# Two transformer layers on one core: the first weight cast ahead of the turned rows, powers ahead of masks, and the division of one late unit ahead of all else

## The chip, the cores and the metric

The kernel runs on 1 core of one Trainium2 chip (trn2). A core has TensorE (PE, with its weight loads shown apart as PEld), VectorE (DVE), ScalarE (ACT), GpSimd (POOL) and SyncE (SP, which here only issues DMAs). Each of these engines takes its own list of instructions strictly in order; between engines they wait for each other through semaphores. The metric is the device time of one execution in microseconds, the median of several runs.

## The reference

An input of 2048 rows by 640 columns goes twice through attention and a dense block with the same weights:

```python
x = A_x
x = x + _A_ref(_layernorm(x, axis=-1), A_wqkv, A_wo)
x = x + _B_ref(_layernorm(x, axis=-1), B_w1, B_b1, B_w2, B_b2)
x = x + _A_ref(_layernorm(x, axis=-1), A_wqkv, A_wo)
x = x + _B_ref(_layernorm(x, axis=-1), B_w1, B_b1, B_w2, B_b2)
```

`_A_ref` makes q, k and v of 32 heads (20 columns each) with one 640x1920 product, takes a softmax over a causal window of 256 positions, and multiplies the heads' sums by `wo` (640x640). `_B_ref` is a 640x1536 product, a bias, a squared relu, a 1536x640 product and a bias. Everything is float32 outside; the kernel splits each operand of a large product into a high and a low float16 part and adds three products of them (high-high, high-low, low-high).

## The kernel before

**Units.** The rows are cut into 8 groups of 256, so two layers are 16 units, numbered 0 to 15. A unit's attention is worked in 8 quads of four heads; a quad has a pass for the row maxima (L888 or L705, reduced on DVE by L722), a pass of scores (L737 or L842), four exponentials on ACT (L827), masks on POOL (L856, four to a quad) and on DVE (L865, two), and products with v (L933), whose tile is copied out by ACT (L945) and DVE (L948).

**Dense work between quads.** While unit u's quads run, PE fills the time between them with `dense`: the products of unit u-1 that are left (the `wo` product of `stage_o`, the normalisation and turning of `stage_y`, then `stage_f` with 12 chunks of the first product, named `y,w_s`, and four groups of 36 matmuls of the second, named `w_s,hh`) and the q, k, v products of unit u+1. In the last unit, 15, only the rest of unit 14's work is left to fill with; a reserve of it is meant for the time after the last quad, when unit 15's own sums come back from DRAM (`load_o`), are multiplied by `wo` and are normalised.

**What sets the order.** The kernel is scheduled by hand at build time. Every piece of work for ACT ("A"), DVE ("D"), POOL ("G") and SP ("S") is posted as a job with a cost in ns, the jobs that it depends on, and a priority; `post` inserts it in a list sorted by priority (0 first), and `pump` takes the first job of that list that could start within 250 ns of the plan's clock. The plan's clock and the costs are the planner's own guesses; the instructions come out in the order of the plan, and the chip then waits wherever the guess was wrong. PE's order is decided by the same plan: dense work is put in until the plan says that the jobs a quad waits for are done. A job's cost or priority therefore also moves matmuls, far from the place where it was changed. For a DMA, the plan adds a landing time to the transfer (`LAND` 1800 ns, `WLAND` 4500 ns).

**What the change touches.** `load_wq` (L278 to L291) issues nine loads of the 640x1920 weight on SP's queue, and casts each 128 columns to a high part on ACT (L272) and a low part on DVE (L273). `layernorm` (L359 to L381) makes statistics on DVE (L366, L370, L371), a power -0.5 on POOL (L377), and the normalised row on DVE (L379); `split_t` turns the rows on PE (L404) and splits them with a cast on ACT (L390) and a subtraction on DVE (L391). `load_o` (L969 to L1034) reads the sums of a unit back and, for each quarter of its rows, makes a reciprocal (L1017), a product (L1020), a cast on ACT (L1024) and a subtraction (L1027), all named by the tiles `ov` and `od` in the last two units. The product with `wo` needs the first two quarters for its first 30 matmuls and the last two for the other 30; L1056 adds its result to x.

**PSUM.** The tiles `acc`, `tr` and `pv` of PE share two buffers (`mm_tile`, tag "mm"), taken in turn: a new one waits until ACT or DVE has read the tile before last. At the kernel's start and in unit 15, the turned rows use the banks of the quads (`bb`) instead.

Of the kernel before, what the change touches and what calls it, by code (L numbers as in the profile page):

```python
# [14 lines left out]
ALU = mybir.AluOpType  # L15

P = 128
Q = P // 2
S = 2048
D = 640  # L20
# [6 lines left out]
NU = NL * NG  # L27
KC = D // P
# [17 lines left out]
def kernel(ctx: ExitStack, tc: tile.TileContext, x, wqkv, wo, w1, b1, w2, b2, out):  # L46
# [60 lines left out]
    def set_row(i, k):  # L107
        nc.vector.memset(krow[i][:, 512 * k:512 * (k + 1)], PAIR)
# [8 lines left out]
    LOOK, LAT, LAND, CROSS, WLAND = 250.0, 50.0, 1800.0, 3600.0, 4500.0  # L117
# [27 lines left out]
    def post(eng, cost, fn, *deps, wait=0.0, prio=1, **kw):  # L145

        j = Job(eng, cost, fn, [d for d in deps if d is not None], now[0] + wait, prio, **kw)
        k = len(pend)
        while k and pend[k - 1].prio > prio:
            k -= 1  # L150
        pend.insert(k, j)
        return j
# [5 lines left out]
    def dma(fn, size, *deps, n=1, cost=450.0, prio=1, **kw):  # L158

        return post("S", n * cost, fn, *deps, prio=prio, size=size, **kw)  # L160
# [109 lines left out]
    def convert(st, hi, low, n, load, *deps, prio=2):  # L270

        a = post("A", 20 + 0.9 * n, lambda: nc.scalar.activation(hi, st, AF.Copy, scale=WS), load, *deps, prio=prio)  # L272
        return post("D", 30 + 1.04 * n, lambda: nc.vector.scalar_tensor_tensor(low, st, WS, hi, op0=ALU.mult,  # L273
                                                                               op1=ALU.subtract), a, prio=prio)
# [3 lines left out]
    def load_wq():  # L278
        at = 0
        for lo, n in [(j * D + c, min(2 * P, D - c)) for c in (0, 2 * P, 4 * P) for j in range(2)] + [  # L280
                (2 * D + c, min(2 * P, D - c)) for c in (0, 2 * P, 4 * P)]:
            raw, o = (w1raw, at) if at + KC * n <= FC * D else (krow[2], at - FC * D)
            at += KC * n
            st = raw[:, o:o + KC * n].rearrange("p (c n) -> p c n", c=KC)
            load = dma(lambda st=st, lo=lo, n=n:
                       nc.sync.dma_start(st, wqkv[:, lo:lo + n].rearrange("(c p) n -> p c n", p=P)),
                       P * KC * n * 4, prio=0, land=WLAND)
            for z in range(0, n, P):
                c = slice(lo + z, lo + z + P)
                wqj[(lo + z) // P] = convert(st[:, :, z:z + P], wq_s[:, 0, :, c], wq_s[:, 1, :, c], KC * P, load,  # L290
                                             prio=1)  # L291

    rowset = {}

# [64 lines left out]
    def layernorm(src, y, *deps, prio=2):  # L359

        box = {}

        def stats(i):
            if i == 0:
                box["st"] = sb.tile([P, 2, 6], F32, name="bst", bufs=2)
            nc.vector.bn_stats(box["st"][:, i, :], src[:, i * HD:(i + 1) * HD])  # L366

        def var():
            box["mv"] = mv = sb.tile([P, 4], F32, name="bmv", bufs=2)
            nc.vector.bn_aggr(mv[:, 0:2], box["st"])  # L370
            nc.vector.tensor_scalar(mv[:, 2:3], mv[:, 1:2], 1e-5, YS ** -2, op0=ALU.add, op1=ALU.mult)  # L371

        j = None
        for i in range(2):
            j = post("D", 455, lambda i=i: stats(i), j, *(deps[i:i + 1] or deps), prio=prio)
        j = post("D", 400, var, j, prio=prio)
        j = post("G", 520, lambda: nc.gpsimd.tensor_tensor(box["mv"][:, 3:4], box["mv"][:, 2:3], neghalf,  # L377
                                                                   op=ALU.pow), j, prio=prio)
        j = post("D", 576, lambda: nc.vector.tensor_scalar(y, src, box["mv"][:, 0:1], box["mv"][:, 3:4],  # L379
                                                           op0=ALU.subtract, op1=ALU.mult), j, prio=prio)  # L380
        return j  # L381
# [34 lines left out]
    def xsrc(l, b):  # L416
        return x_rows[b * P:(b + 1) * P, :] if l == 0 else xs[b]
# [7 lines left out]
    def ln_load(u, *deps, prio=2):  # L425

        l, g = divmod(u, NG)
        ys = []
        for i in range(2):
            xt = sb.tile([P, D], F32, name="xt", tag="xt", bufs=2)  # L430
            load = dma(lambda xt=xt, i=i: nc.sync.dma_start(xt, xsrc(l, 2 * g + i)), P * D * 4, *deps, prio=min(prio, 1))
            ys.append((xt, layernorm(xt, xt, load, prio=prio)))
        lns[u] = ys
# [535 lines left out]
    def load_o(u, late=False, free_=()):  # L969

        l, g = divmod(u, NG)
        opened0.clear()
        if late:
            val = sb.tile([P, KC, T], F32, name="ov", tag="qt", bufs=2)
            od = sb.tile([P, KC, 2, T], F16, name="od", tag="yT", bufs=1)
        else:
            raw = sb.tile([P, 2, KC, T], F32, name="od", tag="hh", bufs=1)
            val = raw[:, 0]
            od = raw[:, 1].rearrange("p c n -> p (c n)").bitcast(F16).rearrange("p (c a n) -> p c a n", a=2, n=T)
        wrote = [ojobs.pop((u, qd)) for qd in range(1, NQ, 2)]  # L980
        rs = sb.tile([P, T], F32, name="rs", bufs=1)

        def load():
            nc.sync.dma_start(rs, ods[u][:, DH:DH + 1].to_broadcast([H, 4, T]))
            nc.sync.dma_start(val.rearrange("p c n -> p (c n)"), ods[u][:, :DH].rearrange("h (d c) n -> h d (c n)", d=4))

        loaded = dma(load, P * (KC + 1) * T * 4, *wrote, *free_, n=2, prio=0)
        if u == NU - 1:
            both = sb.tile([P, 2, D], F32, name="x1", tag="qt", bufs=2)
            x1 = [both[:, i] for i in range(2)]  # L990
        elif u == NU - 2:

            x1 = [krow[(u - 1) % 3][:, i * D:(i + 1) * D] for i in range(2)]
        else:
            x1 = [sb.tile([P, D], F32, name="x1", bufs=2) for i in range(2)]
        xj = {}

        def load_x(i, *deps):
            xj[i] = dma(lambda: nc.sync.dma_start(x1[i], xsrc(l, 2 * g + i)), P * D * 4, *deps, prio=2)

        for i in range(2):

            k = 2 * u + i - 2
            if k < 0 or u >= NU - 2:
                load_x(i, *([loaded] if u == 0 else wrote if u == NU - 1 else ()))
            elif k < len(stored):
                load_x(i, stored[k])
            else:
                waiting[k] = lambda k=k, i=i: load_x(i, stored[k])


        js = []
        for i in range(4):
            q = slice(i * T // 4, (i + 1) * T // 4)

            def ratio(q=q):
                nc.vector.reciprocal(rs[:, q], rs[:, q])  # L1017

            def times(q=q):
                nc.vector.tensor_tensor(val[:, :, q], val[:, :, q],  # L1020
                                        rs[:, q].unsqueeze(1).to_broadcast([P, KC, T // 4]), op=ALU.mult)

            def high(q=q):
                nc.scalar.copy(od[:, :, 0, q], val[:, :, q])  # L1024

            def low(q=q):
                nc.vector.tensor_sub(od[:, :, 1, q], val[:, :, q], od[:, :, 0, q])  # L1027

            pr = urgency["od"]
            j = post("D", 575, ratio, loaded, prio=pr)  # L1030
            j = post("D", 409, times, j, prio=pr)
            j = post("A", 360, high, j, prio=0 if i < 2 else pr)
            js.append(post("D", 402, low, j, prio=pr))
        ols[u] = od, x1, js, xj  # L1034
        if u == NU - 2:
            opened.end = now[0]
        if u == 0:
            rowset[2] = [post("D", 460, lambda k=k: set_row(2, k), *[w2j[c] for c in (7, 8, 9, 10, 11)], prio=2) for k in range(4)]
            for j, load_ in held:
                load_(loaded, *(rowset[2] if j else ()))  # L1040
# [291 lines left out]
    spin(14)  # L1332
    ln_load(0, prio=0)
    load_wq()
    run(ln_t(0))
    spin(7)
# [25 lines left out]
    for n in range(NQ):  # L1362
        todo += [("s", n)] + ([("r", n + LEAD - GQ)] if n % GQ == 1 else []) + [("m", n + LEAD), ("v", n)]
    flow(todo, rest)
    load_o(0)
    dma(lambda: nc.sync.dma_start(b1s, b1.rearrange("(c p) -> p c", p=P)), 8192, *ols[0][2], prio=2)
    b2load = [dma(lambda: nc.sync.dma_start(b2s, bass.AP(tensor=b2.tensor, offset=b2.offset, ap=[[0, P], [1, D]])),
# [60 lines left out]
```

## Time and profile before

| what | value |
|---|---|
| median of 3 runs | 1554.59 us (1553.53 to 1555.71) |
| the profiled execution, its own time | 1555.59 us |
| its span, first to last instruction | 1553.9 us |
| PE busy | 1530.8 us, 25832 matmuls |
| DVE, ACT, POOL busy | 1036.8, 670.0, 453.0 us |
| mean granted clock of PE | 0.998 |

Times in a timeline are microseconds from the span's start; a row gives start, length, engine, line, operation, tiles, and in brackets how long the engine was idle before it and what ended that. In a table of waits a row says who waited for whom, in total, how often, and the longest. In a table of windows each engine's busy time stands with its number of instructions, then the clock that PE was granted (1.00 is full, 0.50 half) and what the DMA engines moved.

### The profile page before, as it was taken

The page shows a single profiled execution, that of the slowest core. Times are in us where ns is not written, and L with a number is a line of the kernel's source. Part 1 is how long each engine was busy: PE and PEld are TensorE (multiplying, and loading weights), DVE is VectorE, ACT ScalarE, POOL GpSimd, SP SyncE. Part 2 cuts the span into 40 slices and gives each one's busy share as a digit, 9 for nine tenths or more (in the row PEclk, how much of TensorE's full clock was granted, in tenths as well). Part 3 has the DMA queues.
Part 4 walks back from the last instruction along what each step waited for, and adds up shares of the span by engine and source line. Part 5 has one row for each costly group of instructions (what it writes and reads, how often), then busy time and mean ns, then how long its engine had stood idle before and what let it go on. Part 6 is the DMA issues. An engine that isn't in the chain of part 4 may idle for free.

```text
span 1553.9 us, 58533 instructions
## 1 busy us (share of the span) xinstructions
PE 1530.8 (99%) x25832; PEld 1197.5 (77%) x25832; DVE 1036.8 (67%) x2246; ACT 670.0 (43%) x1367; POOL 453.0 (29%) x847
## 2 busy tenths in 40 slices
PE   8998999999999999999999999999999999999999
PEld 7766778787787877778777787877878777786777
DVE  8788775666766567665656767667665676767641
ACT  4564445344443534534343443444435345354422
POOL 1223314133231322314132241332314224142321
PEclk9999999999999999999999999999999999999999
DMA  9773353442534334343353434435343352432010
GB/s 283 206 224 100 78 130 86 117 101 80 127 69 125 86 105 114 61 128 79 110 130 65 122 82 130 89 81 128 67 131 79 104 121 62 121 86 64 27 62 18
DMA packets 240343, 162.34 MB, mean 104 GB/s; under 512 B 93016, under 2 KB 224088, under 8 KB 240088
## 3 DMA queue, kind: packets, MB, share of 16 engines
q1 hardware_dynamic: 234136, 149.09, 38.0%
q10 hardware_dynamic: 5952, 9.50, 2.1%
q8 instruction: 203, 3.33, 0.9%
q14 instruction: 52, 0.43, 0.1%
HBM read 79.76 MB, written 58.72 MB: 89 GB/s over the span
## 4 chain that ended last, share of the span: by engine, by line
PE 94%; DVE 3%; ACT 1%; issue 1%; POOL 0%; ACTq 0%; DVEq 0%; POOLq 0%
PE acc L340 74%; PE pv L933 8%; PE bb L705 5%; PE bb L842 5%; PE bb L933 2%; ACT pt L827 1%; DVE mx L722 1%; DVE bb L685 0%; PE bb L737 0%; PE bb L888 0%; DVE bb L719 0%; DVE qd L538 0%; POOL pt L856 0%; PE tr L404 0%; DVE mx L685 0%
## 5 line engine op out<-in xcount | busy, mean ns | idle before, releaser
L827 ACT ACTIVATE pt<-bb 128x640 f32<-128x640 f32 (+2 forms) x512 | 312.5, 683 | 164.7 <-PE bb L842 141.0
L856 POOL TENSOR_SCALAR_AFFINE_SELECT pt<-pt 64x256 f32<-64x256 f32 x448 | 198.5, 443 | 595.9 <-ACT pt L827 566.7
L340 PE MATMUL acc<-y,w_s 128*128 128x256 f16 x2880 | 330.3, 273 | 2.3 <-DVE y L391 2.1
L340 PE MATMUL acc<-w_s,hh 128*128 128x320 f16 (+1 forms) x2340 | 326.7, 297 | 0.1
L340 PEld LDWEIGHTS <-w_s 128*128 128x128 f16 x2880 | 276.2, 98 | 42.1 <-issue 3.2
L340 PEld LDWEIGHTS <-hh 128*128 128x128 f16 x2340 | 222.1, 98 | 86.8 <-issue 0.4
L722 DVE TENSOR_REDUCE mx<-bb 128x4 f32<-128x1024 f32 x224 | 273.1, 1223 | 6.7
L340 PE MATMUL acc<-yT,wq_s 128*128 128x256 f16 x2250 | 259.0, 273 | 2.4 <-DVE mT L797 0.7
L340 PEld LDWEIGHTS <-wq_s 128*128 128x128 f16 x2400 | 229.6, 98 | 36.5 <-issue 3.4
L865 DVE COPY_PREDICATED_SCALAR pt<-drop,zero 128x256 f32 x224 | 99.8, 498 | 138.9 <-ACT pt L827 138.6
L1121 POOL TENSOR_TENSOR r<-r 128x256 f32<-128x256 f32 x192 | 122.6, 659 | 214.6 <-ACT r L1117 212.0
L945 ACT COPY ot<-pv 128x256 f32<-128x256 f32 x128 | 47.7, 372 | 287.5 <-PE bb L933 255.3
L933 PE MATMUL pv<-pt,vt 64*32 64x128 f32 (+5 forms) x3840 | 168.1, 303 | 0.9 <-ACT vt L624 0.9
L1127 DVE TENSOR_TENSOR hh<-r,hh 128x256 f16<-128x256 f32 x192 | 90.5, 484 | 108.7 <-ACT hh L1124 104.3
L933 PE MATMUL bb<-pt,vt 64*32 64x192 f32 (+3 forms) x3584 | 154.6, 302 | 0.4 <-POOL pt L856 0.4
L719 DVE COPY_PREDICATED bb<-maskq,bb 128x256 f32<-128x256 uint16 x224 | 94.0, 424 | 84.8 <-PE bb L705 84.1
L933 PEld LDWEIGHTS pv<-pt,vt 64*32 64x32 f32 (+1 forms) x3840 | 126.1, 106 | 31.5 <-issue 3.3
L340 PE MATMUL acc<-wo_s,od 128*128 128x320 f16 x960 | 139.6, 300 | 2.1 <-ACT od L1024 2.0
L340 PE MATMUL acc<-wq_s,yT 128*128 128x320 f16 x900 | 130.4, 299 | 1.6 <-DVE kt L391 0.5
L1117 ACT ACTIVATE r<-acc,b1s 128x256 f32<-128x256 f32 x192 | 81.2, 477 | 95.3 <-PE acc L340 93.4
L340 PEld LDWEIGHTS <-od 128*128 128x128 f16 x960 | 91.1, 98 | 40.4 <-ACT od L1024 2.3
L933 PEld LDWEIGHTS bb<-pt,vt 64*32 64x32 f32 x3584 | 116.3, 106 | 1.6 <-POOL pt L856 0.9
(105 smaller groups left out, 1444.8 us busy)
## 6 DMA issues: line engine op xcount, KB each, us to landing
o<-ot SPq DMA_DIRECT2D x64, 256.0 KB
qt<-qk SPq DMA_DIRECT2D x30, 480.0 KB
kt<-qk SPq DMA_DIRECT2D x30, 480.0 KB
qk<-qd SPq DMA_DIRECT2D x15, 640.0 KB
od<-o SPq DMA_DIRECT2D x14, 640.0 KB
qk<-yl SPq DMA_DIRECT2D x13, 640.0 KB
xt<-in_A_x_dram SPq DMA_DIRECT2D x16, 320.0 KB
x<-in_A_x_dram SPq DMA_DIRECT2D x16, 320.0 KB
```

The costliest lines, as they stand in the source:

```text
L340: nc.tensor.matmul(acc, lhs(a, c), rhs(b, c), start=(k == 0), stop=(k == 3 * nk - 1))
L705: nc.tensor.matmul(flat[e][rows, o:o + b - a], qt[r, p, i * P + 64 * h:i * P + 64 * (h + 1)], kt[r, p, a + to:b + to], start=True, stop=Tr ...
L719: nc.vector.copy_predicated(wins[:, :, 4 * Q:], later, wins[:, :, :Q])
L722: nc.vector.tensor_reduce(most, wins[:, :, Q:], axis=mybir.AxisListType.X, op=ALU.max)
L827: return lambda: nc.scalar.activation(room_of(box)[:, a:b], bank[:, a:b], AF.Exp, scale=SCALE / (QS * QS))
L842: nc.tensor.matmul(flat[e][h * Q:(h + 1) * Q, c0:c1], kt[r, 2 * qd + j, k0:k0 + Q], qt[r, 2 * qd + j, q:q + c1 - c0], start=True, stop=Tru ...
L856: nc.gpsimd.affine_select(out=m, in_=m, pattern=[[0, 4], [-1 if k else 1, Q]], base=0, fill=0.0, compare_op=ALU.is_gt if k else ALU.is_ge, ...
L865: nc.vector.copy_predicated(m, drop[:, k:k + 1, :].bitcast(mybir.dt.uint16).to_broadcast([P, 4, Q]), zero.unsqueeze(1).to_broadcast([P, 4, ...
L933: nc.tensor.matmul(pv[h][32 * jj:32 * (jj + 1), q0 * Q:(q0 + w) * Q], vf[r, c:c + 32], boxes[e]["pt"][r, a:b], start=(k == 0), stop=(k == ...
L1117: nc.scalar.activation(box["r"], acc[:, f, :], AF.Relu, bias=b1s[:, f0 + f:f0 + f + 1], scale=1.0 / (YS * WS))
L1121: nc.gpsimd.tensor_tensor(box["r"], box["r"], box["r"], op=ALU.mult)
L1127: nc.vector.tensor_sub(hh[:, 1, f, :], box["r"], hh[:, 0, f, :])
```

## The change

Four numbers of the plan are changed. (1) The plan takes the first of the nine weight loads to land 1800 ns after its transfer, not 4500, and the casts of its first 128 columns get priority 0, not 1. (2) The power of every normalisation gets priority 0. (3) In unit 14, the last but one, the products `times` and (4) the casts `high` of the divided sums get priority 0. No instruction's work changes.

```diff
@@ load_wq
-                       P * KC * n * 4, prio=0, land=WLAND)
+                       P * KC * n * 4, prio=0, land=WLAND if at > KC * 2 * P else LAND)
@@
                 wqj[(lo + z) // P] = convert(st[:, :, z:z + P], wq_s[:, 0, :, c], wq_s[:, 1, :, c], KC * P, load,
-                                             prio=1)
+                                             prio=0 if lo + z < P else 1)
@@ layernorm
         j = post("G", 520, lambda: nc.gpsimd.tensor_tensor(box["mv"][:, 3:4], box["mv"][:, 2:3], neghalf,
-                                                                   op=ALU.pow), j, prio=prio)
+                                                                   op=ALU.pow), j, prio=0)
@@ load_o
-            j = post("D", 409, times, j, prio=pr)
-            j = post("A", 360, high, j, prio=0 if i < 2 else pr)
+            j = post("D", 409, times, j, prio=0 if u == NU - 2 else pr)
+            j = post("A", 360, high, j, prio=0 if i < 2 or u == NU - 2 else pr)
```

**At the start, on ACT.** L390 casts the turned rows of unit 0 (out of the banks `bb_143` and `bb_144`), L272 casts weights. Before:

```order
L390 ACT_TABLE_LOAD
L390 CAST yT<-bb_143 128x3x128
L390 CAST yT<-bb_143 128x2x128
L390 CAST yT<-bb_144 128x3x128
L390 CAST yT<-bb_144 128x2x128
L272 ACTIVATE wq_s<-w_s 128x5x128 x6
```

Changed:

```order
L272 ACT_TABLE_LOAD
L272 ACTIVATE wq_s<-w_s 128x5x128 x2
L390 CAST yT<-bb_143 128x3x128
L390 CAST yT<-bb_143 128x2x128
L390 CAST yT<-bb_144 128x3x128
L390 CAST yT<-bb_144 128x2x128
L272 ACTIVATE wq_s<-w_s 128x5x128 x3
```

Both casts of the first weight load now stand ahead of all four casts of the turned rows. On DVE the first low part (L273) likewise stands ahead of the four subtractions L391.

**Unit 14's division, on ACT.** L1024 is the cast of a quarter, L827 an exponential, L945 the copy of a quad's sums. Before:

```order
L1024 CAST od<-ov 128x5x64
L827 ACTIVATE pt<-bb_143 128x640 x2
L1024 CAST od<-ov 128x5x64
L827 ACTIVATE pt<-bb_144 128x640 x2
L1024 CAST od<-ov 128x5x64
L945 COPY ot<-pv 128x256
L827 ACTIVATE pt<-bb_143 128x640 x2
L827 ACTIVATE pt<-bb_144 128x640
L1024 CAST od<-ov 128x5x64
```

Changed:

```order
L1024 CAST od<-ov 128x5x64
L827 ACTIVATE pt<-bb_143 128x640
L1024 CAST od<-ov 128x5x64
L827 ACTIVATE pt<-bb_143 128x640
L827 ACTIVATE pt<-bb_144 128x640
L1024 CAST od<-ov 128x5x64
L827 ACTIVATE pt<-bb_144 128x640
L1024 CAST od<-ov 128x5x64
L945 COPY ot<-pv 128x256
```

All four casts now lie within the exponentials of one quad; the last stood behind three exponentials of the next. From here on the plan also deals PE's dense work out otherwise: before the last quad's `pv` of unit 15 stood 8 matmuls `w_s,hh`, now 48 stand there (8, 8 and 32); between that `pv` and the product with `wo` stood 100 and now stand 96; behind the product with `wo` stood 16, 12 and 8, now none.

**Behind unit 15's product with `wo`, on PE and DVE.** L404 turns the two normalised tiles of unit 15. PE before, around the first of the two:

```order
L340 LDWEIGHTS hh
L340 MATMUL acc<-w_s,hh 128x320
L404 MATMUL bb_143<-ident,xt 128x128 x5
L340 LDWEIGHTS hh
L340 MATMUL acc<-w_s,hh 128x320
```

PE changed:

```order
L340 LDWEIGHTS od
L340 MATMUL acc<-wo_s,od 128x320
L404 MATMUL bb_143<-ident,xt 128x128 x5
L404 MATMUL bb_144<-ident,xt 128x128 x5
L340 LDWEIGHTS w_s
L340 MATMUL acc<-y_28442,w_s 128x256
```

DVE before, from the last addition of that product (L1056) on:

```order
L1056 SCALAR_TENSOR_TENSOR x_28193<-acc,x_28193 128x320
L366 BN_STATS bst<-x_28193 128x6 x2
L370 BN_AGGR bmv<-bst 128x2
L371 TENSOR_SCALAR bmv<-bmv 128x1
L379 TENSOR_SCALAR xt<-x_28193,bmv 128x640
L391 TENSOR_TENSOR y_28428<-bb_143,y_28428 128x3x128
L391 TENSOR_TENSOR y_28428<-bb_143,y_28428 128x2x128
L391 TENSOR_TENSOR y_28428<-bb_144,y_28428 128x3x128
```

DVE changed:

```order
L1056 SCALAR_TENSOR_TENSOR x_28238<-acc,x_28238 128x320
L366 BN_STATS bst<-x_28238 128x6 x2
L391 TENSOR_TENSOR y_28442<-bb_143,y_28442 128x3x128
L391 TENSOR_TENSOR y_28442<-bb_143,y_28442 128x2x128
L370 BN_AGGR bmv<-bst 128x2
L371 TENSOR_SCALAR bmv<-bmv 128x1
L379 TENSOR_SCALAR xt<-x_28238,bmv 128x640
L391 TENSOR_TENSOR y_28442<-bb_144,y_28442 128x3x128
```

The 36 matmuls that stood among the turned rows are gone from here, and the two subtractions of the first tile now stand inside the second tile's normalisation.

**In unit 1 and in the units after it.** POOL takes a power after one, two or three masks of a quad where it came after all four. In unit 1 this also moves DVE and PE: L379 of the second tile now comes ahead of the quad's two L865 (it came behind them, L719 and L273), PE turns that tile ahead of the quad's `pv` (it came behind), and DVE takes L865 twice, L719 and L273 between that L379 and the tile's two L391. In units 2 to 13 the order on PE, ACT and DVE is as it was, but for a handful of rows in unit 2.

## The prediction

> **What bounds the kernel now.** The chain of waits comes first: which engine ends last.
>
> ```profile
> PE 94%; DVE 3%; ACT 1%; issue 1%; POOL 0%; ACTq 0%; DVEq 0%; POOLq 0%
> ```
>
> The path is PE itself. A table of windows over the middle units shows how full it is:
>
> ```profile
> 200.00:1340.00 1140.00, 1138.26 (x19868) 894.11 (x19867) 756.38 (x1595) 482.76 (x987) 336.05 (x624) 1.00 0.41 100
> ```
>
> PE is busy for 1138.26 of 1140 us at full clock (first two numbers, and the 1.00). Four edits that only change an order can win or lose there 1.7 us at most. What can move lies at the start, in units 0 and 1, in the last two units and behind the last product. So the next views are PE's waits, first in 1390 to 1554 us, then in 120 to 146 us:
>
> ```profile
> PE acc L340 <- ACT od L1024: 2.0, 1, 2.0
> PE acc L340 <- DVE y L391: 1.2, 1, 1.2
> PE tr L404 <- DVE x L1156: 0.3, 1, 0.3
> ```
>
> ```profile
> PE tr L404 <- DVE xt L379: 1.2, 1, 1.2
> PE acc L340 <- DVE y L391: 0.9, 1, 0.9
> PE bb L933 <- POOL pt L856: 0.4, 1, 0.4
> ```
>
> Unit 14's wait for the casts `od` (2.0 us) is the one at which edits 3 and 4 aim; the waits for L379 and POOL in unit 1 are those at which the power's priority aims. All six make 6.0 us, 0.4% of the time. Behind unit 15's product with `wo` PE waits for nothing.
>
> The last view is PE's clock, in windows of 3.41 us:
>
> ```profile
> 134.68:138.09 3.41, 1.40 (x35) 1.08 (x36) 2.38 (x4) 0.89 (x3) 3.33 (x5) 1.00 0.50 155
> 138.09:141.50 3.41, 2.80 (x14) 1.94 (x14) 3.38 (x6) 1.50 (x3) 1.14 (x2) 0.50 0.06 23
> ...
> 1431.74:1435.16 3.42, 1.43 (x39) 0.63 (x27) 2.14 (x6) 2.76 (x5) 1.22 (x3) 1.00 0.24 81
> 1435.16:1438.57 3.41, 3.35 (x80) 2.24 (x88) 2.84 (x6) 0.08 (x1) 1.24 (x3) 0.50 0.00 0
> 1451.20:1454.63 3.43, 2.22 (x50) 1.74 (x51) 2.04 (x5) 2.75 (x7) 0.20 (x1) 1.00 0.49 177
> ```
>
> Two windows ran at half clock (0.50), each right behind one in which PE was busy for only 1.40 or 1.43 us; behind the window with 2.22 us the clock stayed. A halved window does half its busy time's work, so these two cost 2.80/2 + 3.35/2 = 3.1 us, as much as half of the waits themselves. So a cluster of about 2 us of idle time can cost up to 1.7 us more, depending on where the grid of windows falls.
>
> **A, the start.** ACT now casts the first weights ahead of the turned rows. Nothing of this part is hidden: PE is waiting.
>
> ```profile
> 0.00:4.00 4.00, 2.57 (x12) 2.57 (x13) 2.90 (x17) 1.28 (x1) 3.13 (x14) 1.00 0.50 161
> 4.00:6.40 2.40, 2.40 (x18) 2.31 (x17) 2.30 (x11) 0.00 (x0) 0.95 (x3) 1.00 0.93 285
> ```
>
> ```profile
> 7.86 0.48 ACT L390 CAST yT<-bb 128x384 f16<-128x384 f32 x1 [5.77 <-PE bb L404]
> 8.96 1.03 ACT L390 CAST yT<-bb 128x256 f16<-128x256 f32 x3 [0.62 <-DVE yT L391]
> 9.87 3.26 ACT L272 ACTIVATE wq_s<-w_s 128x640 f16<-128x640 f32 x5
> ```
>
> ```profile
> 8.37 0.56 DVE L391 TENSOR_TENSOR yT<-bb,yT 128x384 f16<-128x384 f32 x1 [0.31 <-ACT yT L390]
> 10.83 1.55 DVE L273 SCALAR_TENSOR_TENSOR wq_s<-w_s,wq_s 128x640 f16<-128x640 f32 x2
> ```
>
> ```profile
> 11.70 1.48 PE L340 MATMUL acc<-yT,wq_s 128*128 128x256 f16 x12 [0.63 <-DVE wq_s L273]
> ```
>
> When do the weights land? Not before 6.4: up to there 161 GB/s x 4.0 + 285 x 2.4 = 1.33 MB had come in, which is both x tiles (0.66 MB) and the first load (0.66 MB). Not after 9.87, where L272 ran without a wait. I take the middle, 8.2. Two casts then take 2 x 0.63 us (3.26 for five, the last one 0.73), so the first L390 starts at 9.5 instead of 7.86. It ends at 9.98, its L391 at 10.57 (0.56), the other three L390 at 11.62 (1.03), the next L391 at 12.21. The product's second and third matmul need that and start at 12.25 and 12.36; the third stood at 11.70, on L273, which is now long done. **+0.66 us.** The general form is landing + 4.15, so 7.55 breaks even. Bounds: for a landing at 6.4 the tiles' own casts decide, and -0.57 is left (what PE waited for L273, less a short rest); at 9.87 it is +2.33. Behind this PE runs full, so the shift carries through.
>
> **B, unit 1.** POOL takes the power after the first mask.
>
> ```profile
> 132.13 2.93 POOL L856 TENSOR_SCALAR_AFFINE_SELECT pt<-pt 64x256 f32<-64x256 f32 x4 [5.24 <-ACT pt L827]
> 135.15 0.55 POOL L377 TENSOR_TENSOR bmv<-bmv,neghalf 128x1 f32<-128x1 f32 x1
> ```
>
> ```profile
> 132.80 0.88 DVE L865 COPY_PREDICATED_SCALAR pt<-drop,zero 128x256 f32 x2
> 133.58 0.43 DVE L719 COPY_PREDICATED bb<-maskq,bb 128x256 f32<-128x256 uint16 x1
> 133.91 0.87 DVE L273 SCALAR_TENSOR_TENSOR w_s<-kt,w_s 128x640 f16<-128x640 f32 x1
> 135.73 1.14 DVE L379 TENSOR_SCALAR xt<-x,bmv 128x640 f32<-128x640 f32 x1 [0.95 <-POOL bmv L377]
> ```
>
> ```profile
> 558.15:559.45 1.30, 1.30 (x64) 1.08 (x64) 1.00 0.63 122
> ```
>
> The first mask ends near 133.2, the power at 133.75, and L379 near 134.5 instead of 136.87. PE, free at 133.44, waits 1.05 us for it and turns the tile. But then comes `pv`, and its buffer is that of the turned rows, so it waits for the tile's subtraction; ahead of that on DVE now stand L865 twice, L719 and L273, 0.88 + 0.43 + 0.87 us. They end at 136.4, the subtraction at 136.9. `pv` waits 1.7 us, runs unbroken in 1.3 to 1.4 (the window of another unit), and the next product starts near 138.3. Before, it was 138.70 (137.02, plus the turns, plus 0.94). **-0.4 us**, between -1.4 (`pv` has a free buffer) and +0.5 (L865 held up by its exponentials). One wait becomes another.
>
> **Units 2 to 13.** Only POOL's order changes:
>
> ```profile
> 553.41 1.85 POOL L856 TENSOR_SCALAR_AFFINE_SELECT pt<-pt 64x256 f32<-64x256 f32 x4 [2.11 <-ACT pt L827]
> 555.35 0.55 POOL L377 TENSOR_TENSOR bmv<-bmv,neghalf 128x1 f32<-128x1 f32 x1
> ```
>
> The last masks are done at 555.26, and come 0.55 later; `pv` starts at 558.15, so 2.3 us hide it. **0**; without that cover, 0.55 a unit.
>
> **C1, unit 14's `od`.** All four casts go into one quad's exponentials.
>
> ```profile
> 1434.17 0.47 ACT L1024 CAST od<-ov 128x320 f16<-128x320 f32 x1
> ...
> 1442.65 2.49 ACT L827 ACTIVATE pt<-bb 128x640 f32<-128x640 f32 x4 [3.03 <-PE bb L842]
> ```
>
> The fourth cast stood behind three exponentials (1434.17); now it is done before its matmuls are due, and the 2.0 us go. But the exponentials it passes come later, and so do others that the plan moves: the turned rows of `y` now wait for a cast behind three exponentials of about 0.6 us (2.49 for four). Followed through the new order, the cast of the first turned blocks ends some 0.19 + 2.1 + 0.48 us behind the quad's scores and its subtraction 0.56 later, with the handing on 3.4 in all, while PE has eight products (1.1 us), the 0.3 for L1156 and five turns (0.7) to do: it waits some 1.15 (1.0 to 1.4 by what one takes for the handing on). With 0.2 of a `pv` for L865, 0.27 for L1156 and 0.42 of a `pv` for an L391 that comes late with it, I have 2.05 in all, against 2.0 + 0.3 + 1.2 = 3.5 before. **-1.5 us**; between -3.5 (all vanish) and -1.0.
>
> **C2, behind unit 15's product with `wo`.** This is the price. The plan spends its reserve early: 40 more `w_s,hh` before the last `pv`, none of the 36 behind the product.
>
> ```profile
> 1483.62:1497.21 13.59, 13.59 (x106) 9.80 (x101) 5.47 (x13) 1.75 (x5) 0.00 (x0) 1.00 0.45 151
> ...
> 1505.36:1511.35 5.99, 5.99 (x49) 4.67 (x47) 4.06 (x9) 1.33 (x3) 3.99 (x5) 1.00 0.00 0
> ```
>
> ```profile
> 1495.94 0.49 DVE L1027 TENSOR_TENSOR od<-ov,od 128x320 f16<-128x320 f32 x1
> ```
>
> ```profile
> L340 PE MATMUL acc<-w_s,hh 128*128 128x320 f16 x36 | 5.4, 299 | 0.0
> ```
>
> ```profile
> 1505.57 0.49 DVE L1056 SCALAR_TENSOR_TENSOR x<-acc,x 128x320 f32<-128x320 f32 x1 [1.03 <-PE acc L340]
> 1505.97 0.88 DVE L366 BATCH_NORM_STATS2 bst<-x 128x6 f32<-128x320 f32 x2
> ...
> 1507.95 1.14 DVE L379 TENSOR_SCALAR xt<-x,bmv 128x640 f32<-128x640 f32 x1 [0.66 <-POOL bmv L377]
> 1510.97 0.56 DVE L391 TENSOR_TENSOR y<-bb,y 128x384 f16<-128x384 f32 x1 [0.56 <-ACT y L390]
> ```
>
> The first window, from the last `pv` to the product with `wo`, holds 100 `w_s,hh`; with 96 it is 4 x 0.136 = 0.54 us shorter. The second quarter of the divided sums was ready at 1496.43, 0.78 us ahead of need, so still no wait. The second window is the cover: 5.99 us between the end of the `wo` product (1505.36) and `y`, filled by 36 matmuls and ten turned blocks. Without the 36, the chain itself sets the time, counted from that end: addition to 0.70, statistics to 1.49, now two subtractions of the first tile ahead of the rest (0.56 + 0.34) to 2.43, the two short ones to 2.7, power to 3.35, L379 to 4.5 (1.14), turns and casts to 6.05, subtraction to 6.64; `y` runs from about 6.56. PE has only the turns to do, 1.12 us. **+5.4 us of idle time.** Bounds: 4.9 (the 36 x 0.136 us that filled it, nothing added to the chain) and 6.0 (everything in series).
>
> **The clock.** Before lost 3.1 us. Unit 14's cluster shrinks, unit 1's stays at about 2.7, the tail gets a stretch of nearly 4 us idle, behind which one window is halved: 1.7 + 1.7 = 3.4, **+0.3**; one to three halved windows make -2.1 to +2.0.
>
> The Trainium skill, "TensorE: Matmul & The Clock Gate", Part 1, halves the clock only after a whole idle window of some 3.4 us. The trace disagrees, since windows with 1.40 and 1.43 us of work were enough; what the time would be by that rule is rival 1.
>
> **The sum.** Idle 0.66 - 0.4 - 1.5 + 5.4 = 4.2, clock 0.3: +4.5 on the profiled execution's 1555.59 gives 1560.1. That execution lies 1.0 above the median of the runs (1554.59), so the forecast is **1559.1 us**.
>
> **The rivals.** (1) *A halving needs a window that is nearly all idle.* Then neither unit 1 nor, with luck of the grid, the tail is halved: +4.2 - 3.1 = +1.1, 1555.7, no change to be told. Against it stand the rows with 1.40 and 1.43; for it, that there are only two of them. (2) *The 36 matmuls covered little*, the other side: PE came to them because it was their turn, and `y` could have started without them, if the chain behind the product took no longer than the turns, 1.1 us. Then the tail costs nothing and only gains stay: -1.2 idle and -1.7 clock (unit 14's window), 1551.7. It decides below 2.3 us of chain; against it, the rows L1056 to L391 run one after another over 5.4 us in the trace. (3) *The first weights land late*, at 9.87: +2.3 instead of +0.66, 1560.8. The row without a wait allows it; the bytes speak for earlier. (4) *Unit 14's wait is not of the cast's place* but of the reciprocals and sums' landing: its 2.0 and its 1.7 of clock stay, about 1562. Against it, the cast row at 1434.17 right behind exponentials.
>
> **How the numbers follow.** Forecast 0.64, rival 1 0.14, rival 2 0.05, rival 3 0.11, rival 4 0.06. Own range of the forecast 1557 to 1561.5, from tail and clock bounds. The range for 8 in 10 takes in part of rival 1 and of 4: 1555.9 to 1562.3. A measurement here tells 0.2%, 3.1 us, from no change. Faster (below 1551.5) needs most of rival 2: 0.04. Within: rival 1, some of 2, and the forecast's lower end: 0.24. Slower (above 1557.7): 0.72.
>
> **What would show it.** Right: PE idle for some 5 us between the `wo` product and `y` in unit 15, no wait for L1024 in unit 14, the first product's third matmul near 12.4, a `pv` in unit 1 that waits for L391. Wrong: `y` starting within 2 us of the `wo` product's end, halved windows gone from the record, or 2 us idle before unit 14's `od` matmuls as now.

## The result and the profile after

| | before | changed |
|---|---|---|
| median of 5 runs | 1554.97 us (1553.53 to 1558.28) | 1566.54 us (1564.74 to 1567.67) |
| ratio of the runs (the two medians alone give 1.0074) | | 1.0068, 95% interval 1.0055 to 1.0082 |
| span of the profiled execution | 1553.9 us | 1565.1 us |
| mean granted clock (before: 29 runs, taken with the experiments; changed: the five) | 0.995 to 0.999 | 0.992 to 0.995 |

The change makes the kernel slower, as forecast, but by 11.6 us (medians; 11.2 in the profiled executions) and not by 4.5: 1566.54 lies outside the range, 1555.9 to 1562.3.

Where the 11.2 us of span went is seen in a table of windows, five stages of before and then of the changed kernel. The first two numbers are the length of the stage and PE's busy time; their difference is PE's idle time. Before:

```profile
0.00:60.00 60.00, 55.20 (x497) 44.90 (x498) 51.95 (x173) 30.20 (x57) 10.97 (x29) 1.00 0.83 245
60.00:200.00 140.00, 131.18 (x2173) 97.78 (x2172) 108.36 (x236) 72.51 (x147) 43.16 (x80) 0.99 0.57 151
...
1340.00:1470.00 130.00, 125.27 (x2451) 96.00 (x2448) 91.64 (x180) 60.38 (x122) 43.66 (x82) 0.99 0.27 69
1470.00:1553.90 83.90, 80.93 (x854) 64.74 (x853) 28.43 (x65) 24.14 (x56) 19.18 (x33) 1.00 0.12 39
```

Changed:

```profile
0.00:60.00 60.00, 52.97 (x433) 42.28 (x434) 46.41 (x153) 25.05 (x47) 8.88 (x25) 0.94 0.74 232
60.00:200.00 140.00, 131.13 (x2156) 97.65 (x2155) 112.37 (x252) 74.54 (x153) 43.09 (x80) 0.98 0.58 148
200.00:1340.00 1140.00, 1137.88 (x19782) 893.96 (x19780) 752.39 (x1589) 484.38 (x989) 335.90 (x628) 1.00 0.41 100
1340.00:1470.00 130.00, 127.35 (x2534) 98.21 (x2535) 95.09 (x187) 57.37 (x118) 40.32 (x76) 1.00 0.29 75
1470.00:1565.10 95.10, 87.27 (x948) 68.71 (x940) 29.53 (x69) 27.32 (x63) 21.77 (x38) 0.96 0.11 37
```

| stage | PE idle before | changed | difference |
|---|---|---|---|
| 0 to 60 us (start) | 4.80 | 7.03 | +2.2 |
| 60 to 200 (unit 1) | 8.82 | 8.87 | +0.05 |
| 200 to 1340 | 1.74 | 2.12 | +0.4 |
| 1340 to 1470 (unit 14) | 4.73 | 2.65 | -2.1 |
| 1470 to the end | 2.97 | 7.83 | +4.9 |
| sum | | | +5.5 |

The stretches are fixed in time, and the changed kernel runs some us behind in most of them, so a row says where idle time lies rather than what one wait is worth; the sum is free of that. The idle time accounts for 5.5 us, near the forecast's 4.2. The rest is the clock: the column behind the engines fell from 1.00 to 0.94 in the first stage and to 0.96 in the last. The windows of 3.41 us on the grid of this execution show it, for the start and for the tail:

```profile
9.37:12.78 3.41, 1.35 (x11) 1.00 (x10) 2.31 (x5) 2.78 (x8) 0.00 (x0) 1.00 1.10 376
12.78:16.20 3.42, 3.31 (x16) 2.37 (x16) 3.31 (x7) 1.35 (x3) 0.00 (x0) 0.50 1.08 351
36.67:40.09 3.42, 1.11 (x14) 0.79 (x13) 2.11 (x10) 1.25 (x4) 0.00 (x0) 1.00 0.65 168
40.09:43.50 3.41, 2.92 (x15) 1.68 (x12) 3.40 (x18) 0.25 (x1) 0.00 (x0) 0.50 1.06 327
...
1514.65:1518.06 3.41, 0.00 (x0) 0.00 (x0) 2.66 (x7) 0.44 (x2) 1.67 (x3) 1.00 0.00 0
1518.06:1521.48 3.42, 2.25 (x9) 1.57 (x10) 0.95 (x3) 0.75 (x2) 2.40 (x3) 0.50 0.01 2
1521.48:1524.89 3.41, 3.41 (x18) 2.43 (x16) 0.00 (x0) 0.00 (x0) 0.00 (x0) 0.50 0.00 0
```

Six windows ran at half clock: the four above and two in unit 1 (139.08 to 145.90, PE busy for 1.40 and 2.69 us). Half of their busy time is lost: 1.65 + 1.46 + 2.05 + 2.83 = 8.0 us against 3.1 before, **+4.9 us**. With the 5.5 of idle time that makes 10.4 of the 11.2; the other 0.8 is in the lengths of records at full clock and I cannot place it. One execution is a sample of the clock. Over all runs its mean fell from 0.9973 (29 of before) to 0.9936 (the five), an estimate of 0.0037 x 1555 = 5.8 us.

PE's waits, up to 60 us and then from 1400 us on:

```profile
PE tr L404 <- DVE kt L391: 2.3, 1, 2.3
PE acc L340 <- ACT yT L390: 1.6, 1, 1.6
...
PE acc L340 <- DVE yT L391: 0.6, 1, 0.6
```

```profile
PE bb L404 <- DVE xt L379: 3.9, 1, 3.9
PE tr L404 <- DVE y L391: 0.9, 1, 0.9
PE acc L340 <- ACT y L390: 0.6, 1, 0.6
PE acc L340 <- DVE y L391: 0.5, 1, 0.5
PE tr L404 <- DVE x L1156: 0.3, 1, 0.3
PE pv L933 <- DVE y L391: 0.2, 1, 0.2
```

Unit 14's wait for L1024 is gone, the tail has 3.9 + 0.6 + 0.5 us, and at the start stands one that the prediction did not have: 2.3 us for an L391 of unit 1's turned rows (before: 0.7). The chain of waits over that stretch, in order of time, says what it is made of:

```profile
32.44 4.90 DMA qk<-stg
37.34 0.02 issue
37.37 0.41 ACTq L301
...
37.88 0.49 ACT kt L390
38.37 0.02 issue
38.39 0.57 DVE kt L391
38.96 0.04 issue
39.01 0.56 PE tr L404 x3
```

ACT's cast L390 stands behind L301, an instruction by which ACT issues the first load of `wo`. L301 must wait for a semaphore of an earlier transfer (the program gives its DMAs eight semaphores in turn, numbers 101, 102 and 104 to 109 in the trace; here L301 waits for 107, that of a store of `stg`, issued at 32.44, that lands at 37.34). ACT runs in order, so the cast waits too: it starts at 37.88, 1.7 us after ACT's last work. Before, L301 stood one place earlier in ACT's list, was issued at 30.89 and waited for 101, that of a store issued at 26.57; no stall shows there.

### The profile page after: what moved, and what is told of

It is laid out like the page before. It is cut to its first block, busy times and chain, and to the rows that moved or that the text cites. A ratio compares the mean times of both kernels' runs of the same rounds, so it can differ in the third digit from the quotient of the medians.

```text
span 1565.1 us, 58546 instructions
## 1 busy us (share of the span) xinstructions
PE 1536.6 (98%) x25832; PEld 1200.8 (77%) x25832; DVE 1035.8 (66%) x2246; ACT 668.7 (43%) x1367; POOL 450.0 (29%) x847
## 4 chain that ended last, share of the span: by engine, by line
PE 92%; DVE 3%; ACT 1%; issue 1%; DMA 1%; SPq 0%; POOL 0%; ACTq 0%; DVEq 0%; POOLq 0%
PE acc L340 72%; PE pv L933 8%; PE bb L842 5%; PE bb L705 5%; PE bb L933 2%; ACT pt L827 1%; DVE mx L722 0%; DMA w_s<-in_A_wqkv_dram 0%; PE bb L888 0%; PE bb L737 0%; DVE bb L685 0%; DMA qk<-stg 0%; DMA xt<-xs 0%; DVE pt L865 0%; DVE bb L719 0%
## 5 line engine op out<-in xcount | busy, mean ns | idle before, releaser
L827 ACT ACTIVATE pt<-bb 128x640 f32<-128x640 f32 (+2 forms) x512 | 312.3, 684 | 169.4 <-PE bb L842 147.0
L865 DVE COPY_PREDICATED_SCALAR pt<-drop,zero 128x256 f32 x224 | 99.8, 497 | 138.4 <-ACT pt L827 138.3
L933 PE MATMUL pv<-pt,vt 64*32 64x192 f32 (+5 forms) x3840 | 168.0, 304 | 2.6 <-DVE y L391 1.7
L945 ACT COPY ot<-pv 128x256 f32<-128x256 f32 x128 | 47.6, 372 | 281.8 <-PE bb L933 252.9
L719 DVE COPY_PREDICATED bb<-maskq,bb 128x256 f32<-128x256 uint16 x224 | 93.9, 424 | 85.3 <-PE bb L705 84.0
```

The source lines that it names most:

```text
L719: nc.vector.copy_predicated(wins[:, :, 4 * Q:], later, wins[:, :, :Q])
L827: return lambda: nc.scalar.activation(room_of(box)[:, a:b], bank[:, a:b], AF.Exp, scale=SCALE / (QS * QS))
L865: nc.vector.copy_predicated(m, drop[:, k:k + 1, :].bitcast(mybir.dt.uint16).to_broadcast([P, 4, Q]), zero.unsqueeze(1).to_broadcast([P, 4, ...
L933: nc.tensor.matmul(pv[h][32 * jj:32 * (jj + 1), q0 * Q:(q0 + w) * Q], vf[r, c:c + 32], boxes[e]["pt"][r, a:b], start=(k == 0), stop=(k == ...
```

## Experiments

The theories. **Clock and stall:** besides the idle time of the prediction, a nearly idle window costs half of the next one's busy time, and the landing time of edit 1 moves L301 into ACT's way. **Idle time alone** (the prediction's sum): the clock is a small term, and the start costs 0.66 us. Runs of before that were taken with them: median 1555.9 us (29 runs) for the first four, 1556.4 (21) for the next four, 1557.6 (12) for the last three.

### The edits one by one

The first alone:

```diff
-                       P * KC * n * 4, prio=0, land=WLAND)
+                       P * KC * n * 4, prio=0, land=WLAND if at > KC * 2 * P else LAND)
-                                             prio=1)
+                                             prio=0 if lo + z < P else 1)
```

> The first edit alone (landing time and priority of the first weight casts). By the sum of the prediction it costs 0.66 us and nothing behind the first product: about 1555.6 us, no difference from before. By the trace of the changed kernel it costs 4 to 6 us (1559 to 1561): PE's third matmul near 12.9 us, then a wait of over 2 us for an L391 near 39 us, since on ACT the issue of a weight load (L301) that waits for a transfer stands ahead of the cast L390, and halved clock windows near 13 and 40 us.

Measured: 1558.05 us, ratio 1.0017 (1.0006 to 1.0029), +2.6 us, less than the 4 to 6 of the one theory and more than the 0.66 of the other. Its 12 runs reach from 1554.19 (mean clock 0.998) to 1563.86 (0.993). In the profiled execution, one of the shortest, no window was halved at the start; its span of 1554.2 us says little of the others. The waits are there all the same, from 8 to 60 us:

```profile
PE tr L404 <- DVE kt L391: 1.7, 1, 1.7
PE acc L340 <- ACT yT L390: 1.1, 1, 1.1
PE acc L340 <- DVE yT L391: 0.6, 1, 0.6
```

So the two waits of the start are edit 1's. That a window is halved behind them in one run and not in another fits the place of the grid: here the window at the start, 8.50 to 11.91, held 2.21 us of work, in the changed kernel 1.35.

The second alone:

```diff
-                                                                   op=ALU.pow), j, prio=prio)
+                                                                   op=ALU.pow), j, prio=0)
```

> The second edit alone (power of every normalisation at priority 0). By the prediction -0.4 us with the clock unchanged; by the trace of the changed kernel about 0, since unit 1's waits only change place. Both say 1553.5 to 1556.5. If the clusters of idle time in unit 1 halve two windows instead of one, up to 1.5 us more.

Measured: 1556.46 us, ratio 1.0009 (1.0000 to 1.0017). In the profiled execution PE is idle for 8.39 us between 60 and 200 us, against 8.82: the -0.4 of the prediction. But behind the cluster three windows in a row ran at half clock:

```profile
128.84:132.25 3.41, 1.05 (x33) 0.66 (x24) 3.11 (x9) 2.68 (x6) 0.35 (x1) 1.00 0.00 0
132.25:135.66 3.41, 2.52 (x42) 1.91 (x41) 2.59 (x6) 0.51 (x2) 3.12 (x6) 0.50 0.64 192
135.66:139.08 3.42, 1.88 (x49) 1.44 (x56) 2.91 (x4) 0.47 (x2) 3.35 (x4) 0.50 0.30 96
139.08:142.49 3.41, 3.41 (x43) 2.37 (x24) 2.67 (x5) 1.63 (x3) 0.00 (x0) 0.50 0.02 5
```

They cost 3.9 us, against 1.4 in the profile of before. That this is the edit's doing is not shown: in the run with the priority of the casts alone (below), where unit 1's order is that of before, three windows in a row ran at half clock too (134.35 to 144.59, PE busy for 2.60, 2.69 and 3.41 us: 4.4 us). How the grid falls on the same waits makes a difference of this size.

The third and fourth alone:

```diff
-            j = post("D", 409, times, j, prio=pr)
-            j = post("A", 360, high, j, prio=0 if i < 2 else pr)
+            j = post("D", 409, times, j, prio=0 if u == NU - 2 else pr)
+            j = post("A", 360, high, j, prio=0 if i < 2 or u == NU - 2 else pr)
```

> The third and fourth edit alone (products and casts of unit 14's divided sums). By the prediction -1.5 us in unit 14 and +5.4 us behind unit 15's product with wo, with the clock +4 in all (1559). By the trace of the changed kernel -2.5 in unit 14, +5 idle behind that product and 2.8 us of two halved windows there: +5 (1559 to 1561). No L301 stall and no late first product.

Measured: 1561.53 us, ratio 1.0041 (1.0029 to 1.0054). Unit 14's and the tail's waits are those of the full change (0.3, 0.9 and 0.2; 3.9, 0.6 and 0.5), and two windows behind the tail's wait were halved. The three ratios add up to 0.17 + 0.09 + 0.41 = 0.67%, the full change has 0.68%: within the 0.2% or so that the intervals leave, the edits do not work on each other.

### The tail: is it the cover?

The third and fourth edit, with a limit on how far the plan may run ahead of its share of dense work in unit 15:

```diff
-                c = s.go()
+                c = s.go() if ahead < most else None
...
-        together(quads, ahead, dense, cost, share, ..., pace=NQ)
+        together(quads, ahead, dense, cost, share, ..., pace=NQ, most=5000 if last else 1e9)
```

> The third and fourth edit, and a limit on how far ahead of its share the plan may deal out dense work in unit 15, so that 108 w_s,hh stand before the product with wo and 36 (16, 12 and 8) behind it, as many as before the change. If the 36 matmuls are the cover whose loss costs the time, the wait of some 5 us and the halved windows behind the product go, and unit 14's gain is left: about 2 us faster than before (1552 to 1553.5). If the normalisation is late for another reason, a wait of several us stays and the time is 1558 or more.

Measured: 1557.40 us, ratio 1.0009 (1.0000 to 1.0018): 4.1 us less than without the limit. The tail's wait is gone (PE idle for 3.3 us from 1470 us on, as against 8.3 in the third run and 3.0 before), and so are its halved windows. The kernel did not become the expected 2 us faster than before, since the limit also holds dense work back near 1440 us: 4 products `w_s,hh` instead of 28 stand ahead of a quad's scores (L842) there. PE's waits from 1400 us on now begin with another, and one window behind it was halved (1.7 us):

```profile
PE bb L842 <- DVE ot L948: 1.8, 1, 1.8
PE acc L340 <- DVE y L391: 0.9, 1, 0.9
PE tr L404 <- DVE x L1156: 0.7, 1, 0.7
```

The cover alone, taken from the kernel before, with nothing else changed:

```diff
-    run(some(dense, 10e3), stage_o(NU - 1), portion(dense, 1.8e3))
-    run(stage_y(NU - 1, portion(dense, 1.6e3), dense), stage_f(NU - 1))
+    run(some(dense, 40e3), stage_o(NU - 1))
+    run(stage_y(NU - 1, dense), stage_f(NU - 1))
```

> The kernel before with all 136 w_s,hh of the reserve ahead of unit 15's product with wo and none of the 36 behind it; nothing in the other units moves. If the loss behind that product is the missing cover, PE waits some 5 us there, two windows are halved (2.8 us), and the time is 6 to 8 us longer than before (1562 to 1564). By the prediction's sum 5.4 + 0 to 1.7 us. If the chain of the normalisation hides itself, no more than 1 us.

Measured: 1564.69 us, ratio 1.0051 (1.0037 to 1.0065), +7 us. PE's waits from 1500 us on are the very ones of the change:

```profile
PE bb L404 <- DVE xt L379: 3.9, 1, 3.9
PE acc L340 <- ACT y L390: 0.6, 1, 0.6
PE acc L340 <- DVE y L391: 0.5, 1, 0.5
```

That is 5.0 us of waiting, and 2.3 us of halved windows behind it. Where 36 matmuls stand is worth 0.5% of the kernel.

### The start: is it L301?

The first edit, with the first load of `wo` held back in the plan:

```diff
-... P * n * D * 4, gate0))
+... P * n * D * 4, gate0, wait=24000))
```

> The first edit alone, with the first load of wo (L301, issued by ACT) held back by the plan until behind the four casts of unit 1's turned rows. If PE's wait of 1.7 us near 36 us in the run of the first edit alone comes from L301 standing ahead of the cast and waiting for a transfer, it falls to the 0.7 us of before, and the time by about 1 us (1557). If it comes from the order of matmuls and subtractions, 1.7 us stay.

Measured at the place: PE's wait for that L391 is 0.9 us, against 1.7 in the run of the first edit, where L301 stands ahead of the cast, and ACT casts at 34.37 right behind L624:

```profile
34.03 0.44 ACT L624 ACTIVATE vt<-acc 128x320 f32<-128x320 f32 x1 [2.14 <-PE acc L340]
34.37 0.47 ACT L390 CAST kt<-tr 128x384 f16<-128x384 f32 x1
```

So L301 was the stall: 0.8 us of the wait in the run of the first edit, and by the same reckoning some 1.6 in the changed kernel (an estimate, 2.3 against the 0.7 of before). Half of the 0.8 is lost again at once, since a pass of row maxima (L737) moved behind the next wait, which grew from 0.5 to 0.9 us. The time as a whole says nothing on L301: 1571.10 us, ratio 1.0087 (1.0073 to 1.0102), where 1557 was expected. PE now waits 2.1, 1.7 and 2.1 us between 181 and 210 us, where it had not waited before; that the late loads collide with others there is likely, not shown.

Half of the first edit, the priority without the landing time:

```diff
-                                             prio=1)
+                                             prio=0 if lo + z < P else 1)
```

> Half of the first edit: priority 0 for the casts of the first 128 columns, with the landing time of the plan as before. PE's order is that of before; on ACT one weight cast comes ahead of the last cast of the turned rows and the other behind it. If the cost of the first edit is the landing time (both casts ahead of all turned rows, other orders behind), this costs nothing: third matmul between 11.2 and 11.9 us, 1555 to 1556.5. If priority alone does it, the third matmul is near 12.4 us as with the whole edit.

Measured: 1557.64 us, ratio 1.0001 (0.9992 to 1.0011). ACT now puts one weight cast ahead of the last cast of the turned rows, and the third matmul starts at 11.27 instead of 11.70:

```profile
8.96 0.75 ACT L390 CAST yT<-bb 128x256 f16<-128x256 f32 x2 [0.62 <-DVE yT L391]
9.60 0.75 ACT L272 ACTIVATE wq_s<-w_s 128x640 f16<-128x640 f32 x1
```

The weights had landed by 9.60 at the latest. The priority alone is harmless; it takes the landing time as well, by which the plan puts both casts first, to cost something. The landing time without the priority was not run, and the intervals of the two ratios overlap: the rows, not the times, carry this.

### The clock

Idle matmuls in the waits of the changed kernel, 10 more at the start and 26 behind the last product with `wo`:

```diff
-    spin(7)
+    spin(17)
...
+            if u == NU - 1 and i == 0:
+                yield Want()
+                spin(26)
             yield from split_t(y, y2 ...
```

> The changed kernel with idle matmuls (128x128 of the identity, whose result nobody reads) put into two of its waits: 17 instead of 7 ahead of the first product, and 26 between unit 15's product with wo and the turned rows. No other instruction moves. If half clock behind a nearly idle window is a cost of its own, the halved windows near 13 us and near 1518 us go and with them up to 1.65 + 2.8 us: 1562 to 1563.5. If only the waits themselves cost, nothing changes: 1566.5.

Measured: 1570.57 us, ratio 1.0091 (1.0077 to 1.0105), slower than the change itself. I had misplaced one of them and mis-sized both. An idle matmul is 0.23 us, not the 0.14 of a record: each leaves two. The 26 took 5.97 us, and they stood ahead of the first tile's turned blocks. DVE's list then holds everything up:

```profile
1511.83 0.87 DVE L366 BATCH_NORM_STATS2 bst<-x 128x6 f32<-128x320 f32 x2
1518.55 0.89 DVE L391 TENSOR_TENSOR y<-bb,y 128x384 f16<-128x384 f32 x2 [5.85 <-ACT y L390]
1519.36 0.20 DVE L370 BATCH_NORM_AGGREGATE bmv<-bst 128x2 f32<-128x12 f32 x1
```

The second tile's L370 needs only the statistics, ready at 1512.7, but stands behind the two L391 of the first tile, and so PE's wait of 3.87 us came again behind the idle matmuls. At the start the halved window did go: PE passes from the products `yT,wq_s` to `wq_s,yT` at 29.23 instead of 30.95 us, 1.7 us earlier, as much as the halved window had cost.

The same from the other side, in the kernel before:

```diff
+        if n == 13:
+            spin(15)
...
+            if u == 0 and i == 1:
+                yield Want(j)
+                need(j)
+                spin(8)
...
+            if u == NU - 2 and i == 0:
+                yield Want()
+                spin(13)
```

> The kernel before, with idle matmuls in three of its waits: 15 ahead of a pass of row maxima and 8 ahead of a turned tile in unit 1, 13 ahead of unit 14's product with wo. No other instruction moves, but for four rows of DVE. If the clock theory holds, the two halved windows of before (3.1 us) mostly go: 1552.5 to 1554 against 1555.9. If not, no difference.

Measured: 1557.97 us, ratio 1.0011 (1.0002 to 1.0020), at a mean clock of 0.998 to 1.000 in all 11 runs. No window was halved in the profile, but the 36 idle matmuls took 8.7 us of PE (0.24 to 0.26 each), more than the waits in unit 1, and those of unit 14 stood ahead of the wrong half of `od` (its wait is at the third quarter). A full clock that is bought with longer waits gains nothing.

With the sizes right, in the changed kernel (6 at the start, 9 ahead of unit 1's row maxima, 15 behind the first tile's turned blocks):

> The changed kernel with idle matmuls in three waits, each a little shorter than its wait (one took 0.23 to 0.25 us in the runs before): 6 more ahead of the first product, 9 ahead of the pass of row maxima in unit 1, 15 behind the turned blocks of unit 15's first tile. Nothing else moves. If half clock behind a nearly idle window is a cost of its own, no window is halved near 13 us and behind the tail's wait, at most one near 140 us, and the time falls by 3 to 6 us from 1566.5 (1560.5 to 1563.5), with PE's waits of the rest unchanged. If only waits cost, 1566 to 1567.

The edit is the first one of this section with other numbers and another place at the tail (`i == 1` instead of `i == 0`), and the `n == 13` of the second with 9. Measured: 1562.59 us, ratio 1.0038 (1.0025 to 1.0051), against 1.0068 (1.0055 to 1.0082) for the change without them: 0.3%, or 4.7 us by the ratios and 4.0 by the medians. Windows on the grid that the changed kernel had, at its first halved one, and PE at the tail:

```profile
9.37:12.78 3.41, 3.41 (x33) 3.26 (x32) 2.60 (x5) 2.79 (x7) 0.00 (x0) 1.00 1.11 372
12.78:16.20 3.42, 3.42 (x34) 3.07 (x32) 3.22 (x6) 1.29 (x3) 0.00 (x0) 1.00 1.10 377
```

```profile
1511.97 3.51 PE L354 MATMUL spin<-ident 128*128 128x128 f32 x30
1516.01 0.77 PE L404 MATMUL bb<-ident,xt 128*128 128x128 f32 x5 [0.53 <-DVE xt L379]
```

The turned blocks of the second tile still come when the chain of the normalisation ends, 4.6 us after those of the first (before the filling: 1513.59 and 1518.17, also 4.6). The chain is the same, only the clock is kept. Unit 1 went otherwise than expected: with 9 idle matmuls there, two windows near 140 us were halved still (at most one was expected), as was one near 37 us; 4.05 of the 8.0 us of lost work are left.

And in the kernel before, with the harmless half of the first edit:

```diff
-                                             prio=1)
+                                             prio=0 if lo + z < P else 1)
...
+        if n == 13:
+            spin(9)
...
+            if u == 0 and i == 1:
+                yield Want(j)
+                need(j)
+                spin(4)
...
+            if u == NU - 2 and i == 1:
+                yield Want()
+                spin(8)
```

> The kernel before with priority 0 for the first 128 columns' casts and idle matmuls that are shorter than the waits they stand in: 9 and 4 in unit 1, 8 ahead of the third quarter of unit 14's od. By the clock theory no window is halved (before: 3.1 us in the profiled execution) and the first product is 0.4 us earlier: 1552.5 to 1554 against 1556. If the halved windows cost nothing beyond the waits, 1555.5 to 1556.5.

Measured: **1551.92 us** (1551.34 to 1552.68), ratio 0.9968 (0.9956 to 0.9981), clock 0.999 to 1.000 in all five runs: faster than both kernels (those of before taken with it: 1557.57), and steadier than either. Unit 14's wait is filled to a rest of 0.18:

```profile
1429.28 1.95 PE L354 MATMUL spin<-ident 128*128 128x128 f32 x16
1431.41 0.84 PE L340 MATMUL acc<-wo_s,od 128*128 128x320 f16 x3 [0.18 <-ACT od L1026]
```

Since the half edit alone made no difference in time, the gain is that of the filled waits: no halved window is left in the profile, where before had lost 3.1 us. Over the runs the mean clock rose from 0.9968 (the 12 of before) to 0.9998, an estimate of 0.0030 x 1555 = 4.7 of the 5.6 us.

## Why the prediction was wrong in size

**What bounds the kernel: right.** In the middle units nothing moved (+0.4 us of idle time). The 1.7 us of idle time there bound what an order can win, though, not what it can lose: the run with `wo` held back has 7.0. All that the change did lies in the places the prediction named, and a fifth place that it did not.

**A, the start: the price nearly right, what follows from it wrong.** The term was +0.66 for a landing at 8.2; the third matmul started at 12.89, +1.19, within the bounds given. ACT's first row tells when the weights landed in that execution:

```profile
8.87 1.36 ACT L272 ACTIVATE wq_s<-w_s 128x640 f16<-128x640 f32 x2 [6.77 <-DMA w_s<-in_A_wqkv_dram]
```

The prediction's landing + 4.15 gives 13.02 for it. In the run of the first edit L272 starts at 8.36 and the third matmul at 12.38, +0.68. What failed is the sentence "Behind this PE runs full, so the shift carries through". It did not look at the rest of ACT's list: L301 had moved behind another L624 and stalled ACT on a transfer. That added 1.6 us, and idle time there was +2.2 in all. The first edit's cost came with its landing time, through both these ways; its priority alone won 0.4 us of start.

**B, unit 1: right in idle time.** -0.4 forecast, -0.4 measured with the edit alone, and the new wait is that of `pv` for L391 (1.5 us, forecast 1.7). The whole change shows +0.05 there.

**Units 2 to 13: right**, no wait appeared.

**C1, unit 14: right, a little small.** -1.5 forecast, -2.1 measured: the wait for L391 that takes the place of the old ones is 0.9 rather than 1.15, and the `pv` waits are 0.2 in sum rather than 0.6.

**C2, the tail: right.** +5.4 forecast, +4.9 measured, shown twice, by giving the cover back and by taking it alone.

**The clock: the step that failed most.** The term was +0.3, with a bound of +2.0. Measured: +4.9 in the profile, and some 5.8 by the mean clock of all runs. Of the 6.7 us by which the profiled execution misses the sum, 4.6 are this term, 1.3 are idle time (the start +1.6, unit 1 and the middle +0.4 each, units 14 and 15 -1.1), and 0.8 stay open. Three things were missed. The start was not among the places looked at, though its new waits (1.6 and 0.6 us in one window) are as dense as those of unit 1 that the prediction had seen halve a window. Behind the tail two windows were halved and not one, as were two in unit 1. And the term was taken from one execution as if the grid fell alike in the next.

Of the rivals, (1), that a halving needs a nearly idle window, is refuted. In the eleven profiled executions with halved windows, all 29 windows at full clock with at most 1.62 us of work (a run's last one not counted) were followed by one at half clock; of five with 1.76 to 1.85 us three were, and none with 1.98 us or more. By the Trainium skill's rule of a whole idle window ("TensorE: Matmul & The Clock Gate", Part 1) only the tail's would have been halved; the traces disagree. (2), that the 36 covered little, is refuted by the run without cover. (3), a late landing, went a little that way: the weights were there by 8.87 in the profiled execution, between 8.2 and 9.87. (4) is refuted: the wait for L1024 went with the cast's place.

## What to carry to other kernels

On a kernel that keeps TensorE at 99%, count not only the idle time of an edit but where in time it clusters: about 2 us of waits within one window of 3.4 us cost another 1.4 to 4.4 us here, as one to three windows behind it ran at half clock, in places that change from run to run, so that one execution's clock is only a sample. Matmuls that fill such a wait, and are shorter than it, can keep the clock at no cost (all three waits so filled in the kernel before, two of three in the changed one); longer ones give the gain back. And when a planner's guess is changed, follow every engine's list behind that place, the DMA issues in it too: the harm here was done by one issue that moved by one place, and by 36 matmuls that were dealt out too early in a unit that the edit does not name.

## What was not expected of the hardware

- Half clock can last: behind a halved window in which PE was busy for 1.40, 1.88 or 2.52 us at half clock the next was halved too, behind one with 2.69 us in two cases of three, and behind one with 2.80 us or more never; three in a row were seen. At full clock, 1.98 us of work were enough to keep it.
- A DMA issued by ACT waits, in ACT's own list, for the earlier transfer whose semaphore it shares: it held up the cast behind it by 1.7 us, for a store that has nothing to do with it.
- Runs of one kernel differ by their clock: the first edit alone took 1554.19 us at a mean clock of 0.998 and 1563.86 at 0.993.
